# Norm halves, the place of the attention visits and the late stores in a fused attention and MLP kernel

## The chip, the cores and the metric

The kernel runs on one core of a Trainium2 chip. A core has TensorE (PE, matrix products into PSUM), VectorE (DVE), ScalarE (ACT), GpSimd (POOL) and a queue SP that issues the DMAs here. Each engine works through its own queue strictly in order. The metric is the device time of one execution in microseconds (us); lower is better.

## The reference

```python
q_n, k_n = rmsnorm(q, g_q), rmsnorm(k, g_k)       # over D = 64
attn = softmax(q_n @ k_n^T / sqrt(D))             # B, H, S, D = 8, 12, 448, 64
x = (attn @ v) as (B * S, H * D)                  # 3584 x 768
h = x @ w_in                                      # 768 -> 2048
out = (h - tanh(h)) @ w_out                       # 2048 -> 768
```

All of it is in float32; the weights come as float64 and are rounded on the chip.

## The kernel before

**Two streams.** `bounded_path` mixes two streams of work on PE. The attention goes by *slots*, one for each pair of heads: 8 batches with 6 pairs give the slots s = 0 to 47. The MLP is a Python generator `mlp()` that yields after each matmul. A slot calls `run(ns)` between its own steps, which advances the generator by so many planned nanoseconds. So the order of all the work is written out by hand: what is emitted first stands first in each engine's queue.

**The visit.** In slots s >= 12 (`slot`), PE does the attention in one block, called a visit here. `scores(s + 1, KF)` (L568) starts it: 8 matmuls into two of the three score banks (`sc`). Then `visit` interleaves the products of probabilities and values of slot s (L634, L622, into two banks of their own) with the other scores of slot s + 1. Each pair of score banks is read by two exponentials on ACT (L574), into `p_last` first, then `p` and `p_full`. As only three banks rotate, the second bank of the first full score block is the bank that the first `p_last` exponential must have read. `divide` takes the values out: an ACT copy (L754), a DVE add (L755) and a DVE multiply by the reciprocal sums (L756).

**The rest of a slot** is the list `work` of 14 points, with a stretch of MLP before each. For slot s + 1: the probabilities are added up (L599, L605, L612), transposed in 32x32 blocks and reduced (`fold`, `fold_rest`: L709, L716), brought together by eight small ACT copies (`gather`, L724), reduced, inverted, copied to the other partitions, widened and transposed (`spread_sums`, `turn_sums`: L733 to L744). For slot s + 2: q and k are scaled by their norms (L532) and transposed (L542, L546, then an ACT multiply L547). For slot s + 3: squares on ACT (L499), a reduction on DVE (L506), then the two halves of each norm, which lie in neighbouring groups of 32 partitions, are brought together (`meet_blocks`: four ACT copies L513; `meet_rest`: DVE L518 and L519). `power_blocks` (L525, POOL) takes the power -0.5 at the start of the next slot. `load_blocks` issues 8 DMAs for slot s + 4.

**The MLP by products of Strassen type.** The first layer (`hidden`) has 4 *sets* a batch. A set has seven *products* in the order 1, 5, 6, 2, 3, 7, 4, of 6 matmuls each, in three rotating PSUM banks (`mm`): 1, 5, 6 and 4 open a bank; 2, 3 and 7 add to the banks of 1, 5 and 6. In `done_with`/`use`, product 1 is copied out by ACT (L899); 5 and 6 are added to that copy by DVE (L901, L903); product 2 gets a tanh (ACT) and a subtraction (DVE, L880); 3 (L911), 7 (L907, L908) and 4 (L915) are added by DVE, and their tanh (L879) and subtraction (POOL, L880) are emitted after the next product. A bank can be opened again only when its last reader is done.

From batch 2 on two batches go together: `hidden(b)`, two *outer blocks* of `project_pair`, `hidden(b + 1)`, the other five. An outer block is seven products of 4 matmuls and a whole product of 8 double ones: 44 units of the size of one matmul. Before it, POOL makes the operands `u` (L1040) from the first layer's results; after it, DVE combines the results (L1089, the whole one of some blocks by ACT, L1096), partly at once and partly from the list `calm`, one entry a product. In `x_sums` POOL (L788) makes operands `tt` for the first layer from the attention's output.

**The phase.** A slot beside `hidden` has 42 units, one set; the slots beside the first two outer blocks have 44 and beside the others 110. So each visit falls at the same place of a set, and `AHEAD_NS`, added up over the six slots s = 12 to 17, sets that place: 6 units, so that the visit stands after product 1. A pair's slots begin at s = 18, 30 and 42.

**The stores.** `store` transposes a finished piece on DVE (L940) into a buffer `th`, of which there are two, shared with the tanh; the four output DMAs (L945) are issued on SP a product later.

Of the kernel before, what the change touches and what calls it, by code (L numbers as in the profile page):

```python
# [9 lines left out]
F32 = mybir.dt.float32  # L10
# [134 lines left out]
def bounded_path(tc, ctx, q, k, v, moe_w_in, moe_w_out, out, g_col, ident, ones, half_ones, neg_half, early):  # L145
# [20 lines left out]
    P = 128  # L166
# [320 lines left out]
    def load_blocks(s):  # L487
        b, hp = steps[s]
        t = loaded["qk", s] = qk_rows()[:, : 2 * S].rearrange("p (i j d) -> p i j d", i=2, j=NJ)
        for i, src in enumerate((q, k)):  # L490
            for h in range(2):
                rows = src[b, 2 * hp + h].rearrange("(j t) (m d) -> m t j d", t=BL, d=BL)
                for m in range(2):
                    r = (2 * h + m) * BL
                    nc.sync.dma_start(out=t[r : r + BL, i], in_=rows[m])
# [13 lines left out]
    def meet_blocks(s):  # L509

        mine, other = normed["rr", s]
        for g in range(P // BL):
            nc.scalar.copy(out=other[g * BL : (g + 1) * BL], in_=mine[(g ^ 1) * BL : ((g ^ 1) + 1) * BL])  # L513

    def meet_rest(s):

        mine, other = normed["rr", s]
        nc.vector.tensor_tensor(out=mine, in0=mine, in1=other, op=ALU.add)  # L518
        nc.vector.tensor_scalar(out=mine, in0=mine, scalar1=1.0 / D, scalar2=1e-6, op0=ALU.mult, op1=ALU.add)  # L519
        normed["rr", s] = mine  # L520

    def power_blocks(s):

# [79 lines left out]
    def add_third(s):  # L603
        for t in sums[s]:
            nc.vector.tensor_tensor(out=t, in0=t, in1=full(s)[2], op=ALU.add)  # L605
# [122 lines left out]
    def spread_sums(s):  # L728

        acc = whole[s]  # L730
        total = late["blocks"].tile([P, NJ], F32, name="sum_all")
        top = total[: 2 * BL]
        nc.vector.reduce_sum(top, acc.rearrange("p g j -> p j g"), axis=AX.X)  # L733
        nc.vector.reciprocal(top, top)
        for m in range(2):
            nc.vector.tensor_copy(out=total[(2 + m) * BL : (3 + m) * BL], in_=total[m * BL : (m + 1) * BL])
        wide = whole[s] = late["blocks"].tile([P, NJ, BL], F32, name="sum_w")
        nc.vector.tensor_copy(out=wide, in_=total[:, :, None].to_broadcast([P, NJ, BL]))

    def turn_sums(s):  # L740

        wide = whole[s]
        rs = whole[s] = late["blocks"].tile([P, S], F32, name="rs_T")
        nc.vector.transpose(out=rs, in_=wide.rearrange("p j k -> p (j k)"))  # L744

    def divide(s, av):
        b, hp = steps[s]
        rs = whole.pop(s)
        if b > PAIRED and b % 2 and hp == 1:
            x = xT[b, hp] = late["blocks"].tile([P, S], F32, name="xT_more", bufs=1)  # L750
        else:
            x = xT[b, hp] = xp.tile([P, S], F32, name="xT")
        if s >= FOLDED:
            nc.scalar.copy(out=x, in_=av[0][:, :S])  # L754
            nc.vector.tensor_tensor(out=x, in0=x, in1=av[1][:, :S], op=ALU.add)  # L755
            nc.vector.tensor_tensor(out=x, in0=x, in1=rs, op=ALU.mult)  # L756
        for m in range(2):
            rows = slice(m * D, (m + 1) * D)
            for n in range(0 if s >= FOLDED else 2):
                nc.vector.tensor_tensor(  # L760
                    out=x[rows, n * HS : (n + 1) * HS], in0=av[n][rows, :HS], in1=rs[n * D : (n + 1) * D],
                    op=ALU.mult,
                )
        for c in range(NCH):
            del probs[s, c]
        if b < PAIRED and hp >= HC:
            c = hp - HC
            x_sums(b, (c,), range(4), nc.vector if b == 0 and c == HC - 1 else nc.gpsimd)

    def x_sums_later(s, second):  # L770
        b, hp = steps[s]
        for c in {(HC + 1, 0): (0,), (HC + 1, 1): (1,), (HC + 2, 0): (2,)}.get((hp, second), ()):
            x_sums(b, (c,), range(4), nc.gpsimd)

    def x_sums(b, chunks, which, eng):
# [22 lines left out]
    def part(name):  # L798
        return tp.tile([P, 2, HS], F32, name=name)
# [131 lines left out]

        return products(b, 0, SETS, 2, HC, moving, done_with)

    def store(b, n, y):

        o = part("th").rearrange("p f s -> p (f s)")
        nc.vector.transpose(out=o, in_=y if b >= FIRST else y.rearrange("r (c p) -> r p c", c=NCH))  # L940

        def issue():
            for i in range(P // BL):
                d = n * P + i * BL
                nc.sync.dma_start(  # L945
                    out=out[b * S : (b + 1) * S, d : d + BL].rearrange("(j t) d -> t j d", t=BL),
                    in_=o[i * BL : (i + 1) * BL].rearrange("t (j d) -> t j d", d=BL),
                )

        late["out"].append([1 if b >= PAIRED else 2, issue])  # L950
# [103 lines left out]
    def project_pair(b, ks):  # L1054
# [36 lines left out]
        def combine_outer(p, m, y):  # L1091

            e, f = acc[:, m], acc2[:, m]
            if p in (1, 3):
                if m == HC - 1:
                    nc.scalar.copy(out=e if p == 1 else f, in_=y)  # L1096
                return
            third = m == HC - 1
            o = y
            if third and p in (2, 5, 4):  # L1100
                o = f if p == 2 else e if p == 4 else part("s1").rearrange("p f s -> p (f s)")

            def soon(*args):
                if third:
                    add(*args)
                else:
                    calm.append(lambda: add(*args))

            if p == 2:
                soon(o, y, e)  # L1110
                calm.append(lambda: store(b, m, o))
            elif p == 7:
                soon(e, e, y)
                soon(f, f, y, ALU.subtract)
            elif p == 6:
                soon(e, e, y)
            elif p == 5:
                soon(o, y, e)
                calm.append(lambda: add(f, f, o))
                calm.append(lambda: store(b + 1, HC + m, o))  # L1120
                calm.append(lambda: store(b + 1, m, f))
            else:
                soon(o, y, e)
                calm.append(lambda: store(b, HC + m, o))

        def flush():
            now, late["todo"] = late["todo"], []
# [168 lines left out]

    H_NS = 4 * HS / ENGINE_NS * 7 * 6 * SETS
    O_NS = 4 * HS / ENGINE_NS * 7 * HC * HF
    AHEAD_NS = 4 * HS / ENGINE_NS * 6
    OUTER_NS = 4 * HS / ENGINE_NS * (7 * HF // 2 + 2 * HF)  # L1300

    def gap_ns(s):
# [8 lines left out]
    def has(s):  # L1311
        return 0 <= s < NS
# [69 lines left out]
    def slot(s):  # L1382

        gap = gap_ns(s)
        av = av_banks
        if has(s + 1):
            scores(s + 1, KF)
        if s < FOLDED:
            last_values(s, av)
            totals(s, sc_bank())  # L1390
            divide(s, values(s, av))
            for c in range(KF):
                scores(s + 1, c)
        else:
            visit(s, av)
        if has(s + 2):
            load(s + 2, "v")
        rows, ahead, following = has(s + 2), has(s + 3), has(s + 1)
        folded = following and s + 1 >= FOLDED
        first = s + 3 == TURNED  # L1400
        scaled = rows and not first
        if scaled:
            power_blocks(s + 2)
        work = (
            ((following, lambda: add(s + 1, False)), (first, lambda: turn(s + 2, sc_bank(), sc_bank()))),
            ((following, lambda: add_third(s + 1)), (first, lambda: load_blocks(s + 3))),
            ((following, lambda: add_last(s + 1)), (first, lambda: load_blocks(s + 4))),
            ((folded, lambda: fold(s + 1)),),
            ((folded, lambda: fold_rest(s + 1)), (True, lambda: x_sums_later(s, 0))),
            ((scaled, lambda: scale_blocks(s + 2)),),  # L1410
            ((scaled, lambda: turn_blocks(s + 2, 0)), (folded, lambda: gather(s + 1, 0))),
            ((scaled, lambda: turn_blocks(s + 2, 1)), (folded, lambda: gather(s + 1, 1))),
            ((True, lambda: x_sums_later(s, 1)), (has(s + 4) and not first, lambda: load_blocks(s + 4))),
            ((folded, lambda: spread_sums(s + 1)), (ahead, lambda: square_blocks(s + 3))),
            ((folded, lambda: turn_sums(s + 1)),),
            ((ahead, lambda: norm_blocks(s + 3)),),
            ((ahead, lambda: meet_blocks(s + 3)),),
            ((ahead, lambda: meet_rest(s + 3)),),
        )
        for point in work:  # L1420
            run(4 * gap / (len(work) + 1))
            for wanted, fn in point:
                if wanted:
                    fn()
        run(4 * gap / (len(work) + 1))
# [358 lines left out]
```

## Time and profile before

| What | Value |
|---|---|
| Time, median of 3 runs | 1405.35 us (1402.68 to 1407.94) |
| Profiled execution | 1405.19 us |
| Its span (first to last instruction) | 1403.3 us |
| PE busy | 1340.1 us, 95% |
| DVE / POOL / ACT busy | 1014.8 / 720.1 / 535.9 us |
| Mean granted TensorE clock | 0.990 |
| DMA share, 250 to 440 us / 440 to 1230 us | 0.90 / 0.58 |

A row of the timeline has the start in us, the time taken in us, engine, line, operation, what is written and read, and how many; in brackets stands how long the engine was idle before it and what ended that. A row of the waits names the waiting instruction and what it waited for, then the total in us, how often, and the longest. A stretch of the windows view lists the busy time of PE, the weight loads, DVE, ACT and POOL, then the granted clock, the DMA share and GB/s. In the profile a float32 matmul of the MLP appears as two records. PE counts as busy while matmuls are in its pipeline, so short stalls do not all show as idle time.

### The profile page before, as it was taken

What the parts mean: (1) busy time and instruction counts of PE and PEld (TensorE: products, weight loads), DVE (VectorE), ACT (ScalarE), POOL (GpSimd) and SP (SyncE); (2) the same over time, 40 slices, a digit from 0 to 9 for tenths busy, and PEclk for the clock granted to TensorE, in tenths of its full rate; (3) what the DMA queues carried; (4) which work ended last, traced back from release to release, by engine and by line L of the source; (5) the groups of instructions that cost most, each with busy time, mean ns of one, the idle gap of its engine ahead of it and who ended that gap; (6) DMA issues with size and microseconds to landing.
All of it is one profiled execution on the core that took longest, in us unless ns stands there. A gap on an engine that the chain in (4) does not pass through costs nothing.

```text
span 1403.3 us, 29144 instructions
## 1 busy us (share of the span) xinstructions
PE 1340.1 (95%) x11336; PEld 1051.6 (75%) x11336; DVE 1014.8 (72%) x1529; ACT 535.9 (38%) x1291; POOL 720.1 (51%) x409
## 2 busy tenths in 40 slices
PE   7988999999999999999999999999999999999996
PEld 3467854488889886878767788688777788699884
DVE  5999989668656677868886777678796677634563
ACT  7856554343432534353321444344411254311100
POOL 4756666157672439243873336633596134712660
PEclk9999999999999999999999999999999999999998
DMA  7879889889998655565546766375653774455544
GB/s 172 187 213 253 264 239 242 257 258 330 298 277 237 167 152 148 135 163 146 151 119 145 192 161 166 92 178 144 164 160 99 149 196 134 125 152 177 168 140 78
DMA packets 371688, 253.54 MB, mean 181 GB/s; under 512 B 282196, under 2 KB 310228, under 8 KB 371540
## 3 DMA queue, kind: packets, MB, share of 16 engines
q1 hardware_dynamic: 371536, 251.57, 65.8%
q8 instruction: 92, 1.51, 0.4%
q14 instruction: 56, 0.46, 0.1%
q10 hardware_dynamic: 4, 0.00, 0.0%
HBM read 205.23 MB, written 46.27 MB: 179 GB/s over the span
## 4 chain that ended last, share of the span: by engine, by line
PE 65%; DVE 16%; DMA 6%; issue 4%; SPq 4%; ACT 3%; POOL 2%; DVEq 0%; ACTq 0%; POOLq 0%
PE mm L832 26%; PE mm L1082 20%; PE sc L568 8%; PE mm L1246 5%; PE sc L634 4%; DMA out_dram<-th 2%; DMA qk_nat<-in_q_dram 1%; DVE qk_n L532 1%; DVE rows L605 1%; DMA w_f<-w_inner 1%; DVE rr_mine L506 1%; DMA gT<-in_moe_w_in_dram 1%; PE sc L672 1%; SPq L945 1%; DVE w_out L354 1%
## 5 line engine op out<-in xcount | busy, mean ns | idle before, releaser
L832 PE MATMUL mm<-xT,w_f 128*128 128x224 f32 x1296 | 264.0, 353 | 4.1 <-DVE s L1089 3.9
L832 PEld LDWEIGHTS mm<-xT,w_f 128*128 128x128 f32 x1296 | 244.5, 190 | 10.2 <-DVE s L1089 5.4
L568 PE MATMUL sc<-qT,kT 64*32 64x448 f32 (+1 forms) x3072 | 223.5, 502 | 15.6 <-ACT p_last L574 14.4
L832 PE MATMUL mm<-tt,w_f 128*128 128x224 f32 x1044 | 209.5, 355 | 0.7 <-DVE g L880 0.7
L525 POOL TENSOR_TENSOR rr_mine<-rr_mine,neg_half 128x28 f32<-128x28 f32 x33 | 160.4, 4860 | 94.5 <-DVE rr_mine L519 42.3
L832 PEld LDWEIGHTS mm<-tt,w_f 128*128 128x128 f32 x1044 | 195.7, 190 | 16.8 <-issue 15.4
L880 POOL TENSOR_TENSOR gT<-s,th 128x448 f32<-128x448 f32 x60 | 73.4, 1225 | 193.7 <-ACT th L879 193.7
L568 PEld LDWEIGHTS sc<-qT,kT 64*32 64x32 f32 x3072 | 76.0, 106 | 92.5 <-issue 44.6
L1082 PE MATMUL mm<-u,w_f 128*128 128x224 f32 x672 | 138.8, 358 | 4.6 <-DVE acc L1089 2.3
L1082 PEld LDWEIGHTS mm<-u,w_f 128*128 128x128 f32 x672 | 126.9, 192 | 13.5 <-issue 11.9
L880 POOL TENSOR_TENSOR g<-s,th 128x448 f32<-128x448 f32 x36 | 45.8, 1275 | 171.2 <-ACT th L879 171.2
L1082 PE MATMUL mm<-gT,w_f 128*128 128x224 f32 (+1 forms) x480 | 131.6, 427 | 0.0
L634 PE MATMUL sc<-p,v_nat 64*32 64x448 f32 x1120 | 130.9, 544 | 0.0
L1082 PEld LDWEIGHTS mm<-gT,w_f 128*128 128x128 f32 x480 | 90.9, 190 | 34.7 <-issue 34.0
L1082 PE MATMUL mm<-g,w_f 128*128 128x224 f32 (+1 forms) x360 | 100.7, 433 | 5.7 <-DVE s L1089 5.7
L755 DVE TENSOR_TENSOR xT<-xT,sc 128x448 f32<-128x448 f32 x32 | 19.8, 618 | 117.5 <-PE sc L568 72.6
L1082 PEld LDWEIGHTS mm<-g,w_f 128*128 128x128 f32 x360 | 69.0, 193 | 33.7 <-issue 26.7
L574 ACT ACTIVATE p<-sc 128x448 f32<-128x448 f32 x132 | 72.1, 546 | 37.5 <-PE sc L568 34.3
L724 ACT COPY sum_g<-sum 32x14 f32<-32x14 f32 x280 | 56.3, 201 | 78.0 <-DVE sum L716 72.1
L879 ACT ACTIVATE th<-s 128x448 f32<-128x448 f32 x96 | 55.0, 573 | 61.5 <-DVE s L907 21.2
L879 ACT ACTIVATE th<-mm 128x448 f32<-128x448 f32 x32 | 17.4, 543 | 155.7 <-PE mm L832 149.8
L1246 PE MATMUL mm<-gT,w_out 128*128 128x448 f32 x192 | 74.3, 542 | 0.0
(186 smaller groups left out, 2451.4 us busy)
## 6 DMA issues: line engine op xcount, KB each, us to landing
w_f<-w_in SPq DMA_DIRECT2D x196, 384.0 KB, 3.8
w_f<-w_inner SPq DMA_DIRECT2D x63, 512.0 KB, 3.6
w_f<-w_out SPq DMA_DIRECT2D x42, 512.0 KB, 4.1
w_raw<-in_moe_w_out_dram SPq DMA_DIRECT2D x16, 768.0 KB, 5.4
out_dram<-th SPq DMA_DIRECT2D x192, 56.0 KB, 2.7
w_in<-w_out SPq DMA_DIRECT2D x21, 384.0 KB, 5.4
qk_nat<-in_q_dram SPq DMA_DIRECT2D x132, 56.0 KB, 2.4
qk_nat<-in_k_dram SPq DMA_DIRECT2D x132, 56.0 KB, 2.3
```

Source lines behind the costliest of these rows:

```text
L354: nc.vector.tensor_tensor(out=dst, in0=x, in1=y, op=op)
L525: nc.gpsimd.tensor_tensor(out=mine, in0=mine, in1=neg_half[:, :1].to_broadcast([P, 2 * NJ]), op=ALU.pow)
L568: nc.tensor.matmul(tiles[h][i * BL : (i + 1) * BL, :n], lhsT=kT[r, c * P + at : c * P + at + BL], rhs=qT[r, first : first + n], start=True ...
L574: nc.scalar.activation(p[:, h, c if c < 2 else 0, :], tiles[h][:, :n], AF.Exp, scale=1.0 if rr is None else rr[:, 0, 2 * c + h : 2 * c + h ...
L634: nc.tensor.matmul(av[g][i * BL : (i + 1) * BL, :S], lhsT=v_nat[keys, h, c, m * BL : (m + 1) * BL], rhs=p[keys, h], start=first, stop=True ...
L724: nc.scalar.copy(out=acc[h * BL : (h + 1) * BL, g], in_=part[g * BL : (g + 1) * BL, h * NJ : (h + 1) * NJ])
L755: nc.vector.tensor_tensor(out=x, in0=x, in1=av[1][:, :S], op=ALU.add)
L832: nc.tensor.matmul(bank[:, f * HS : (f + 1) * HS], lhsT=w[:, c * width + f, :], rhs=moving[p](c), start=(first and f == 0 and c == 0), sto ...
L879: nc.scalar.activation(th, h, AF.Tanh, bias=0.0, scale=1.0)
L880: eng.tensor_tensor(out=g[:, rows, cols], in0=h, in1=th, op=ALU.subtract)
L1082: nc.tensor.matmul(bank[:, :n], lhsT=w(i), rhs=mv, start=(first and i == 0), stop=(i == len(moving) - 1), skip_group_check=not first,)
L1246: nc.tensor.matmul(bank[:, :S], lhsT=w_out_row(f, n // HC)[:, n % HC * P : (n % HC + 1) * P], rhs=g[:, f, :], start=(f == 0), stop=(f == C ...
```

## The change

- `meet_blocks`: instead of four ACT copies and one DVE add, DVE adds each group of 32 partitions to its neighbour directly, four adds into `rr_other`; the scaling follows at once. `meet_rest` is gone.
- `spread_sums`: the sums stay on 64 partitions and are no longer copied to the other 64 (two DVE copies less). The widening becomes `widen_sums`, on ACT and over 64 partitions. `divide` multiplies the two halves of x separately.
- In `work`, the squares stay beside `spread_sums`, one point sooner; the reduction and the norm halves come one point sooner in the list, and the transpose of the sums goes behind them. `load_blocks` goes one point later, the POOL sums of x move to other points, and the last point is empty.
- `AHEAD_NS` goes from 6 to 18 units: the MLP is 12 units further at each visit from s = 18 on, so that the visit stands after products 1, 5 and 6.
- `store` can be given another buffer: in block 5 every second store writes into the piece `o` that has just been stored, in block 4 (the last) every store writes into an accumulator that is no longer needed. `th` is used for the others.

```diff
         for g in range(P // BL):
-            nc.scalar.copy(out=other[g * BL : (g + 1) * BL], in_=mine[(g ^ 1) * BL : ((g ^ 1) + 1) * BL])
-
-    def meet_rest(s):
-
-        mine, other = normed["rr", s]
-        nc.vector.tensor_tensor(out=mine, in0=mine, in1=other, op=ALU.add)
-        nc.vector.tensor_scalar(out=mine, in0=mine, scalar1=1.0 / D, scalar2=1e-6, op0=ALU.mult, op1=ALU.add)
-        normed["rr", s] = mine
+            own, met = slice(g * BL, (g + 1) * BL), slice((g ^ 1) * BL, ((g ^ 1) + 1) * BL)
+            nc.vector.tensor_tensor(out=other[own], in0=mine[own], in1=mine[met], op=ALU.add)
+        nc.vector.tensor_scalar(out=other, in0=other, scalar1=1.0 / D, scalar2=1e-6, op0=ALU.mult, op1=ALU.add)
+        normed["rr", s] = other
...
-        total = late["blocks"].tile([P, NJ], F32, name="sum_all")
-        top = total[: 2 * BL]
-        nc.vector.reduce_sum(top, acc.rearrange("p g j -> p j g"), axis=AX.X)
-        nc.vector.reciprocal(top, top)
-        for m in range(2):
-            nc.vector.tensor_copy(out=total[(2 + m) * BL : (3 + m) * BL], in_=total[m * BL : (m + 1) * BL])
-        wide = whole[s] = late["blocks"].tile([P, NJ, BL], F32, name="sum_w")
-        nc.vector.tensor_copy(out=wide, in_=total[:, :, None].to_broadcast([P, NJ, BL]))
+        total = whole[s] = late["blocks"].tile([2 * BL, NJ], F32, name="sum_all")
+        nc.vector.reduce_sum(total, acc.rearrange("p g j -> p j g"), axis=AX.X)
+        nc.vector.reciprocal(total, total)
+
+    def widen_sums(s):
+
+        total = whole[s]
+        wide = whole[s] = late["blocks"].tile([2 * BL, NJ, BL], F32, name="sum_w")
+        nc.scalar.copy(out=wide, in_=total[:, :, None].to_broadcast([2 * BL, NJ, BL]))
...
-            nc.vector.tensor_tensor(out=x, in0=x, in1=rs, op=ALU.mult)
         for m in range(2):
             rows = slice(m * D, (m + 1) * D)
+            if s >= FOLDED:
+                nc.vector.tensor_tensor(out=x[rows], in0=x[rows], in1=rs, op=ALU.mult)
+                continue
...
-        for c in {(HC + 1, 0): (0,), (HC + 1, 1): (1,), (HC + 2, 0): (2,)}.get((hp, second), ()):
+        for c in {(HC + 1, 1): (0,), (HC + 1, 2): (1,), (HC + 2, 0): (2,)}.get((hp, second), ()):
...
-    def store(b, n, y):
+    def store(b, n, y, o=None):
...
-        o = part("th").rearrange("p f s -> p (f s)")
+        if o is None:
+            o = part("th").rearrange("p f s -> p (f s)")
...
-                calm.append(lambda: store(b + 1, m, f))
+                calm.append(lambda: store(b + 1, m, f, o))
             else:
                 soon(o, y, e)
-                calm.append(lambda: store(b, HC + m, o))
+                calm.append(lambda: store(b, HC + m, o, f if third else e))
...
-    AHEAD_NS = 4 * HS / ENGINE_NS * 6
+    AHEAD_NS = 4 * HS / ENGINE_NS * 18
...
-            ((following, lambda: add_third(s + 1)), (first, lambda: load_blocks(s + 3))),
+            (
+                (following, lambda: add_third(s + 1)), (first, lambda: load_blocks(s + 3)),
+                (True, lambda: x_sums_later(s, 0)),
+            ),
...
-            ((folded, lambda: fold_rest(s + 1)), (True, lambda: x_sums_later(s, 0))),
+            ((folded, lambda: fold_rest(s + 1)), (True, lambda: x_sums_later(s, 1))),
...
-            ((True, lambda: x_sums_later(s, 1)), (has(s + 4) and not first, lambda: load_blocks(s + 4))),
             ((folded, lambda: spread_sums(s + 1)), (ahead, lambda: square_blocks(s + 3))),
-            ((folded, lambda: turn_sums(s + 1)),),
+            (
+                (has(s + 4) and not first, lambda: load_blocks(s + 4)), (True, lambda: x_sums_later(s, 2)),
+                (folded, lambda: widen_sums(s + 1)),
+            ),
             ((ahead, lambda: norm_blocks(s + 3)),),
             ((ahead, lambda: meet_blocks(s + 3)),),
-            ((ahead, lambda: meet_rest(s + 3)),),
+            ((folded, lambda: turn_sums(s + 1)),),
+            (),
         )
```

## The prediction

> **What bounds the kernel now.** I read the page first, then who TensorE (PE) waited for, then the timelines around one wait. The profiled execution took 1405.19 us, 1403.3 of it span; the median shown is 1405.35, so the sum below, made against the profiled run, can be read against the median too.
>
> ```profile
> span 1403.3 us, 29144 instructions
> PE 1340.1 (95%) x11336; PEld 1051.6 (75%) x11336; DVE 1014.8 (72%) x1529; ACT 535.9 (38%) x1291; POOL 720.1 (51%) x409
> ```
>
> PE is the bound, so only its stalls can be won. The waits of PE inside 440 to 1230 us, where attention (batches 3 to 7) and the MLP pairs interleave:
>
> ```profile
> PE sc L568 <- ACT p_last L574: 13.1, 11, 2.7
> PE mm L1082 <- DVE s L1089: 5.7, 2, 2.9
> PE mm L832 <- DVE s L1089: 3.9, 2, 2.4
> PE mm L1082 <- DVE s L908: 2.0, 3, 0.7
> ```
>
> That view undercounts, since weight loads move ahead. So I took each visit in PE's timeline from its first score matmul to the next product. Visits that nothing disturbs take 5.43 us (772.34 to 777.77). Numbering visits by s, with s=18 at 440.33, those of s=19 to 46 exceed 5.43 by 33.7 us in all: 0.6 to 0.8 behind the easy sets, 1.8 to 2.2 behind the fourth, 3.6 and 5.3 at s=23 and s=35. Why, in the visit that starts at 506.42 (ACT's timeline, then PE's):
>
> ```profile
> 505.88 0.58 ACT L879 ACTIVATE th<-s 128x448 f32<-128x448 f32 x1 [0.55 <-DVE s L907]
> 507.87 0.91 ACT L513 COPY rr_other<-rr_mine 32x28 f32<-32x28 f32 x4 [1.41 <-DVE rr_mine L506]
> 508.81 0.58 ACT L879 ACTIVATE th<-s 128x448 f32<-128x448 f32 x1
> 509.29 0.51 ACT L899 COPY s<-mm 128x448 f32<-128x448 f32 x1
> 509.70 0.61 ACT L574 ACTIVATE p_last<-sc 128x224 f32<-128x224 f32 x2
> ...
> 508.00 1.24 PE L634 MATMUL sc<-p,v_nat 64*32 64x448 f32 x3
> 510.12 0.56 PE L568 MATMUL sc<-qT,kT 64*32 64x448 f32 x1 [0.88 <-ACT p_last L574]
> ```
>
> The scores were ready at 506.9, but the exps stand in ACT's queue behind four norm copies, which wait for DVE's L506, then the tanh of product 4 and the copy of product 1. PE has three score banks, needs the first one back 1.9 us into the visit, and stops.
>
> **The change, part by part.** Times are from the visit's end, V. A hidden slot holds 42 matmuls of 0.383 us (7 products of 2.3) and a visit: 21.5 us undisturbed. I lay the new order of each engine's queue with the durations of the slot that starts at 490.33.
>
> *Norm halves on DVE, sooner.* ACT loses 4 x 0.23 us and the wait before them; DVE gets four 32x28 adds for one. Not in the trace: the nearest are L518 (128x28 add, 0.19) and L736 (32x14 copy, 0.17), so 0.7 for four, net +0.5; bounds 0.2 (pipelined) and 4.3 (each as L518's worst, 1.09). I take 0.7: they now stand before product 5's add, where nothing on PE is near.
>
> *Sums.* DVE loses two copies (2 x 0.19) and the widening L738 (0.3 to 0.4); ACT gets a 64x448 copy, 0.53 as L754; the multiply by the sums becomes two of 64 rows, each priced as L756 (0.55 start to start; bounds 0.3 and, blocked like the L605 of 2.14, 1.6). Net on DVE per slot with the norm: about +0.3.
>
> *Visits behind three products.* The MLP runs 12 matmuls further before each visit from s=18 on; total PE work is unchanged. DVE in the new order: division 0.1 to 1.85; L599's add to 2.95; the tanh difference L880 at 3.05; the three sum adds 3.6 to 6.0; product 3's add 6.0; transpose and reduction 6.55 to 8.7; scaling to 9.7; product 7's two adds to 10.85; two transposes to 11.95; product 4's add to 12.5. ACT: kT 12.05, gather to 13.65, tanh, square, widening, tanh, and product 1's copy ends at 16.8. The visit starts at 16.1, and PE needs the first exp done at 18.0; it is done at 17.3. So the stall goes. What is late next is the mm banks: product 5 of the next set (11.5) needs product 7's reads, done 10.85, a margin of 0.65; product 6 (13.8) has 1.3. Before, the visit lay between and gave 5.4 us more. When POOL stretches one DVE op by a us, as in the third line here, that margin is gone:
>
> ```profile
> 491.07 0.62 DVE L756 TENSOR_TENSOR xT<-xT,rs_T 128x448 f32<-128x448 f32 x1
> 491.61 1.08 DVE L599 TENSOR_TENSOR rows<-p 128x896 f32<-128x896 f32 x1
> 493.45 2.14 DVE L605 TENSOR_TENSOR rows<-rows,p_full 128x896 f32<-128x896 f32 x1
> ```
>
> I leave 0.25 us a visit on 22 visits, 5.5 of 33.7 (bounds 0 and 12). Gain 28.2.
>
> L605 ran beside POOL's 2.67 us L1040, but L756 and L599 ran at full speed beside POOL's 4.78 us power L525 (487.23 to 492.01). The Trainium skill, "SBUF — State Buffer" (SBUF: two separate sides), says that a DVE op with two SBUF inputs and a GpSimd op that reads SBUF exclude each other for a whole instruction, which speaks against the added adds and the second multiply. By it L756 would have waited 0.94 us here for the power to end; an estimate from that is 25 us over 27 slots, and the sum would be 1408. By the rows the multiplies lose nothing beside a power, and I keep that.
>
> *Where sets meet the outer products the shift costs.* Three places, two times each.
> At s=27 and 39 the fourth set of the second batch is followed directly by products 1, 5, 6 of the third outer block. Product 6 multiplies the u made by POOL (L1040, 2.1) from the difference L880 (1.14) of product 7, whose tanh stands in ACT's queue behind the gather: 13.65 + 0.56 + 1.15 + 2.1 = 17.6 with waits. Product 6 is due at 9.2 + 3.06 = 12.3. Before, the u ended at 674.33 while the visit lasted to 677.98:
>
> ```profile
> 672.23 2.10 POOL L1040 TENSOR_TENSOR u<-g,u 128x896 f32<-128x896 f32 x1
> 674.29 1.13 POOL L880 TENSOR_TENSOR g<-s,th 128x448 f32<-128x448 f32 x1
> ```
>
> That is 5.3 us of stall, twice. Long stalls also cost clock: after the 2.85 us wait that ended at 1052.36 the windows view shows
>
> ```profile
> 1052.00:1058.00 6.00, 5.64 (x15) 5.14 (x16) 4.09 (x9) 1.19 (x5) 0.95 (x1) 0.50 0.46 126
> ```
>
> a granted clock of 0.50 for 6 us, 3.4 us lost; after the 2.8 us stall at 887 about 1.7; after those at 555 and 715 nothing. I add 2.5 to each 5.3: 15.6 in all (bounds 0 and 20). The Trainium skill, "TensorE: Matmul & The Clock Gate" (Part 1: The HAM clock gate), has the clock halved after an idle window of about 3.4 us; by that the two 2.8 us stalls should not have halved it, and they did.
> At s=22 and 34, the whole product's copy L1096 frees a bank that product 6 of the next block wants at 13.0; it now stands behind gather, square and widening and ends at 15.3: 2.3 twice, 4.6 (bounds 0 and 7).
> At s=23 and 35 the same bank waits for a DVE add behind the gather, 15.9 against 14.55: 1.35 twice, 2.7 (bounds 0 and 6).
>
> *Elsewhere outside visits.* The long outer slots lost 10.2 us: twice 3.02 at 715 and 1049, behind DVE ops of 2 to 3 us beside POOL, 0.7 for a u, and the 3.4 of clock. DVE drops 2.85 us of copies and transpose just before, and L506 moves behind the add that PE waited for; I leave 2.7, gain 7.5 (bounds 0 and 10). Five small waits on L908 and L880, 3.5 us, become 1.0: gain 2.5.
>
> *Half the late stores elsewhere.* Stores shared two th buffers, and DVE waited for their DMAs: `DVE th L940 <- DMA out_dram<-th: 31.8, 14, 7.0` in DVE's waits. PE paid 1.72 at 768 and 2.55 at 1104; with six of twelve stores a pair in finished tiles this goes: gain 4.3 (bounds 0 and 4.3). After PE's end DVE wrote its last transpose at 1395.2 after a 1.2 us wait; without the waits it can end 4 us sooner, but SP issues four DMAs a store at 0.5 us each and can hold that: gain 3 (0 to 5). The moved block loads are 8 DMAs on SP one point later; PE waited for no DMA in this stage, where DMA is 58% busy, so I price them at nothing; if that cover ended, the next slot's L499 would wait for them, a slot later. x sums moved on POOL: the last chunk's first subtraction needs no new x, so it stays ahead of product 5.
>
> Sum: 28.2 + 7.5 + 2.5 + 4.3 + 3 = 45.5 gained; 15.6 + 4.6 + 2.7 = 22.9 lost; 1405.2 - 22.6 = 1382.6, say 1383.
>
> **The rivals.**
> *Slower: DVE's bank margin.* At product 5 of each next set the two multiplies, the adds and the POOL overlaps delay product 7's reads by more than 0.65 us. Each us beyond costs 22 us. Above 1.7 us of delay the net gain is gone; at 2.4 us the time is 1383 + 22 x 1.75 = 1421. For it: the 2.14 us L605. Against: slots 19 and 21 show no such op in that stretch.
> *The visits stay held.* ACT still runs tanh, square and the new widening shortly before the exps (0.7 us margin). If DVE is 1 us later than laid, a third to a half of the visit gain stays lost: 1383 + 14 = 1397.
> *The stalls where sets meet do not bite* because tanh and u come earlier than laid: without most of the 22.9 it is 1365. Against: the queue order is fixed and the old slot shows the same gather end (13.5).
> *No change*, 1405: the wins and the new stalls cancel fully, each within its bounds.
>
> **How the numbers follow.** Forecast 0.50 (own range 1374 to 1392), visits held 0.20 (1392 to 1402), no stalls at the meeting 0.15 (1358 to 1374), no change 0.06, bank-bound 0.09. The measurement tells about 0.5%, 7 us, from no change: below 1398.3 lie 0.50 + 0.15 + 0.14 = 0.79, within 0.06 + 0.06 = 0.12, above 0.09. The range 1364 to 1402 leaves out part of the third case and all slower ones.
>
> **What would show it.** Right: visits of s=19 to 26 near 5.43 us, no wait on p_last above 0.5; L513's wait for L506 gone; PE waits of 4 to 6 us for POOL's u at two places about 330 us apart, ahead of the visits s=28 and 40; fewer waits of L940 for DMAs. Wrong: PE waiting for DVE's L907 or L908 once per set (the bank rival), or p_last still in PE's list with about 13 us.

## The result and the profile after

The changed kernel takes 1419.01 us (median of 4 runs, 1416.28 to 1419.78) against 1405.01 us; the ratio is 1.0095, with a 95% interval of 1.0072 to 1.0118. It is slower by 14 us, where 22.6 us less were forecast. The profiled execution has a span of 1417.3 us, 14.0 more than before. Its page says:

```profile
span 1417.3 us, 29026 instructions
PE 1338.8 (94%) x11336; PEld 1044.0 (74%) x11336; DVE 1063.2 (75%) x1558; ACT 525.6 (37%) x1194; POOL 720.1 (51%) x409
```

PE has no more work than before, so the 14 us are waits and slow clock. These are PE's waits inside 440 to 1260 us (lines move by 1 to 5 against before: the adds of product 7 are L906 and L907, the adds of the probabilities L595, L601 and L608, the scaling L528, the gather L720, the widening L735, the tanh L878, the whole product's copy still L1096):

```profile
PE mm L1082 <- issue: 16.7, 3, 6.5
PE mm L1082 <- POOL u L1040: 10.9, 2, 5.5
PE mm L1082 <- DVE s L907: 7.0, 5, 2.1
PE mm L1082 <- DVE s L1089: 3.0, 4, 1.0
PE mm L831 <- DVE acc L1089: 2.7, 2, 1.4
PE mm L1082 <- ACT s L1156: 2.1, 2, 1.9
```

The waits on `p_last`, 13.1 us before, are gone. In their place stand few and long waits at L1082, the outer products. The visits themselves are free: those of s=19 to 46 exceed 5.43 us by 0.6 us in all, against 33.7. ACT's timeline at the visit that starts at 512.02 shows why: its queue is through with everything else when the scores arrive.

```profile
511.42 0.57 ACT L878 ACTIVATE th<-s 128x448 f32<-128x448 f32 x1
511.89 0.51 ACT L898 COPY s<-mm 128x448 f32<-128x448 f32 x1
512.77 0.61 ACT L570 ACTIVATE p_last<-sc 128x224 f32<-128x224 f32 x2 [0.37 <-PE sc L564]
```

Where the time went is told by the distances from one visit's start to the next. The third column is what 42 or 44 units of 0.383 us and a visit of 5.43 us take:

| Slots s | Before, us | Undisturbed | After, us |
|---|---|---|---|
| Inside sets (15 slots) | 336.4 | 322.8 | 323.5 |
| 28, 29, 40, 41 (long outer slots) | 204.8 | | 194.3 |
| 21, 33, 45 (sets end, outer block 1 begins) | 70.9 | 64.6 | 78.8 |
| 22, 34, 46 (outer block 2 begins) | 70.2 | 66.8 | 93.0 |
| 23, 35 (outer block 2 ends) | 53.5 | 44.6 | 47.7 |
| 27, 39 (sets end, outer block 3 begins) | 49.4 | 43.0 | 61.2 |

The last four rows stand 61.7 us above undisturbed after the change, 25.0 before. At s=22 the timelines of DVE, ACT and PE read:

```profile
547.16 3.00 DVE L601 TENSOR_TENSOR rows<-rows,p_full 128x896 f32<-128x896 f32 x1
...
550.68 4.33 DVE L608 TENSOR_TENSOR rows<-rows,p_last 64x448 f32<-64x448 f32 x2
...
557.65 0.88 ACT L720 COPY sum_g<-sum 32x14 f32<-32x14 f32 x4 [12.95 <-DVE sum L712]
...
561.00 0.88 ACT L720 COPY sum_g<-sum 32x14 f32<-32x14 f32 x4
...
562.75 0.55 ACT L735 COPY sum_w<-sum_all 64x448 f32<-64x448 f32 x1
563.21 0.52 ACT L1096 COPY acc<-mm 128x448 f32<-128x448 f32 x1
...
563.83 3.32 PE L1082 MATMUL mm<-u,w_f 128*128 128x224 f32 x8 [6.50 <-issue]
```

PE resumes 0.1 us after L1096 has freed its bank. "issue" hides this: the view names no releaser, but nothing else ends there. L1096 had its input long before; it stands in ACT's queue behind a gather that waits 12.95 us for DVE. At s=27 it is the tanh of product 7 that stands behind the gather, and POOL's chain behind that tanh (ACT, POOL, PE):

```profile
677.44 0.88 ACT L720 COPY sum_g<-sum 32x14 f32<-32x14 f32 x4
678.34 0.58 ACT L878 ACTIVATE th<-s 128x448 f32<-128x448 f32 x1
...
679.00 1.80 POOL L879 TENSOR_TENSOR g<-s,th 128x448 f32<-128x448 f32 x1 [5.68 <-ACT th L878]
680.88 2.07 POOL L1040 TENSOR_TENSOR u<-g,u 128x896 f32<-128x896 f32 x1
...
683.00 1.49 PE L1082 MATMUL mm<-u,w_f 128*128 128x224 f32 x3 [5.46 <-POOL u L1040]
```

And at s=21 DVE's scaling, 1.1 us elsewhere, takes 2.94 beside POOL's u and holds product 7's adds, whose bank PE wants for outer product 5, the second of the block (DVE, PE):

```profile
526.28 2.94 DVE L528 TENSOR_TENSOR qk_n<-qk_nat,rr_other 128x896 f32<-128x896 f32 x1
...
529.67 0.61 DVE L907 TENSOR_TENSOR s<-mm,s 128x448 f32<-128x448 f32 x1
...
530.43 4.95 PE L1082 MATMUL mm<-u,w_f 128*128 128x224 f32 x16 [2.12 <-DVE s L907]
```

Each of the long waits is followed by slow clock. The windows view (duration; PE, weight loads, DVE, ACT, POOL; granted clock, DMA share, GB/s) has, right after the stalls at s=22 and s=27:

```profile
563.80:567.00 3.20, 3.17 (x9) 2.91 (x10) 1.45 (x7) 0.17 (x1) 1.51 (x1) 0.50 0.86 244
682.80:686.00 3.20, 3.00 (x8) 2.75 (x9) 1.93 (x1) 0.00 (x0) 3.20 (x3) 0.50 0.50 133
```

### The profile page after: what moved, and what is told of

It is laid out like the page before. It is cut to its first block, busy times and chain, and to the rows that moved or that the text cites. A ratio compares the mean times of both kernels' runs of the same rounds, so it can differ in the third digit from the quotient of the medians.

```text
span 1417.3 us, 29026 instructions
## 1 busy us (share of the span) xinstructions
PE 1338.8 (94%) x11336; PEld 1044.0 (74%) x11336; DVE 1063.2 (75%) x1558; ACT 525.6 (37%) x1194; POOL 720.1 (51%) x409
## 4 chain that ended last, share of the span: by engine, by line
PE 71%; DVE 14%; POOL 5%; issue 3%; DMA 3%; SPq 1%; ACT 1%; ACTq 0%; DVEq 0%; POOLq 0%
PE mm L831 32%; PE mm L1082 17%; PE sc L564 8%; PE mm L1246 5%; PE sc L630 5%; POOL u L1040 2%; DVE xT L756 1%; PE sc L668 1%; DVE qk_n L528 1%; PE sc L618 1%; POOL tt L787 1%; DVE rows L601 1%; DVE rows L608 1%; POOL rr_other L521 1%; DVE gT L1032 1%
## 5 line engine op out<-in xcount | busy, mean ns | idle before, releaser
L564 PE MATMUL sc<-qT,kT 64*32 64x448 f32 (+1 forms) x3072 | 214.1, 500 | 3.1 <-ACT p_last L570 1.9
L521 POOL TENSOR_TENSOR rr_other<-rr_other,neg_half 128x28 f32<-128x28 f32 x33 | 160.6, 4868 | 102.8 <-DVE rr_other L515 102.8
L1082 PE MATMUL mm<-u,w_f 128*128 128x224 f32 x672 | 146.5, 372 | 35.5 <-issue 16.7
L1082 PEld LDWEIGHTS mm<-u,w_f 128*128 128x128 f32 x672 | 132.6, 200 | 42.5 <-issue 26.7
L1082 PE MATMUL mm<-gT,w_f 128*128 128x224 f32 (+1 forms) x480 | 138.4, 442 | 2.1 <-ACT s L1156 2.1
L1082 PEld LDWEIGHTS mm<-gT,w_f 128*128 128x128 f32 x480 | 94.6, 199 | 42.6 <-issue 38.6
L564 PEld LDWEIGHTS sc<-qT,kT 64*32 64x32 f32 x3072 | 70.8, 106 | 70.8 <-issue 51.7
L630 PE MATMUL sc<-p,v_nat 64*32 64x448 f32 x1120 | 111.4, 536 | 0.0
L1082 PE MATMUL mm<-g,w_f 128*128 128x224 f32 (+1 forms) x360 | 103.1, 439 | 3.5 <-DVE s L1089 3.0
L720 ACT COPY sum_g<-sum 32x14 f32<-32x14 f32 x280 | 56.3, 201 | 121.2 <-DVE sum L712 115.6
L878 ACT ACTIVATE th<-s 128x448 f32<-128x448 f32 x96 | 55.1, 575 | 120.0 <-DVE s L910 95.1
L1082 PEld LDWEIGHTS mm<-g,w_f 128*128 128x128 f32 x360 | 69.9, 197 | 34.0 <-issue 27.8
L570 ACT ACTIVATE p<-sc 128x448 f32<-128x448 f32 x132 | 71.9, 545 | 50.6 <-PE sc L564 37.8
L514 DVE TENSOR_TENSOR rr_other<-rr_mine 32x28 f32<-32x28 f32 x132 | 70.5, 534 | 3.9
```

The source lines that it names most:

```text
L514: nc.vector.tensor_tensor(out=other[own], in0=mine[own], in1=mine[met], op=ALU.add)
L521: nc.gpsimd.tensor_tensor(out=mine, in0=mine, in1=neg_half[:, :1].to_broadcast([P, 2 * NJ]), op=ALU.pow)
L564: nc.tensor.matmul(tiles[h][i * BL : (i + 1) * BL, :n], lhsT=kT[r, c * P + at : c * P + at + BL], rhs=qT[r, first : first + n], start=True ...
L570: nc.scalar.activation(p[:, h, c if c < 2 else 0, :], tiles[h][:, :n], AF.Exp, scale=1.0 if rr is None else rr[:, 0, 2 * c + h : 2 * c + h ...
L630: nc.tensor.matmul(av[g][i * BL : (i + 1) * BL, :S], lhsT=v_nat[keys, h, c, m * BL : (m + 1) * BL], rhs=p[keys, h], start=first, stop=True ...
L720: nc.scalar.copy(out=acc[h * BL : (h + 1) * BL, g], in_=part[g * BL : (g + 1) * BL, h * NJ : (h + 1) * NJ])
```

## The experiments

**Where the visits stand, and the norm halves.** The first theory ("place"): the stalls come from where the visits stand. The rival ("turn-taking"): at s=21 the four norm adds run beside POOL's u's, each add takes turns with one POOL instruction, three u's and a subtraction (0.84, 2.02, 1.08 and 2.03 us; 0.18 for most others), so the power starts late (542.38), the u's behind it fall on L601 and L608 and stretch these. Four kernels were run beside each other, with the kernel before at 1406.61 us.

```diff
# phase6 and phase12, on the changed kernel
-    AHEAD_NS = 4 * HS / ENGINE_NS * 18
+    AHEAD_NS = 4 * HS / ENGINE_NS * 6      # 12 in phase12
# before18, on the kernel before
-    AHEAD_NS = 4 * HS / ENGINE_NS * 6
+    AHEAD_NS = 4 * HS / ENGINE_NS * 18
# copies18, on the changed kernel
-            nc.vector.tensor_tensor(out=other[own], in0=mine[own], in1=mine[met], op=ALU.add)
...
+            nc.scalar.copy(out=other[g * BL : (g + 1) * BL], in_=mine[(g ^ 1) * BL : ((g ^ 1) + 1) * BL])
...
-            ((folded, lambda: turn_sums(s + 1)),),
+            ((folded, lambda: turn_sums(s + 1)), (ahead, lambda: meet_rest(s + 3))),
```

> The changed kernel with the visits put back behind product 1 (6 units), everything else kept. Place theory (the stalls where sets meet outer blocks, 17.6 us at s=27 and 39 and about 24 us at s=22, 34 and 46, come from where the visits stand): these stalls go, the visits are held only in part because the norm copies no longer stand ahead of the exponentials, time 1375 to 1392. Turn-taking theory (the four small norm adds each take turns with one POOL u, the power -0.5 comes 5 us later, and all behind it): the stalls at s=22 and 34 stay for more than half, time 1395 to 1410.

> The changed kernel with the visits behind products 1 and 5 (12 units). Place theory: at s=27 and 39 the visit stands ahead of the product 6 that waited for u, so both stalls of 5.6 us and their 3.2 us of half clock go (17.6); at s=22 and 34 the product 6 of the second outer block still comes ahead of the visit and keeps 4 to 7 us; visits near 5.5 us; time 1395 to 1405. Turn-taking theory: no place of the visits helps at s=22 and 34, and the power is late in the same way; 1400 to 1412.

> The kernel before with only the visits put behind three products (18 units). Place theory: visits near 5.43 us, but 5 to 6 us of stall at s=27 and 39 and 2 to 6 us at s=22 and 34, with their half clock, time 1400 to 1415, above the kernel before or level with it. Turn-taking theory: without the norm adds the power is on time, the stalls at s=22 and 34 are 2.5 us or less, time 1383 to 1395.

> The changed kernel, but the norm halves brought together as before: four ACT copies and one DVE add of 128 partitions, with the scaling one point later. Turn-taking theory: the power of s=21, 33 and 45 starts about 4 us sooner, the DVE adds L601 and L608 behind it run beside it at 1.1 and 0.6 us, and the 6.7 us stalls at s=22 and 34 fall to 2.5 or less, with most of their 3.2 us of half clock: time 1395 to 1402. Place theory: the stalls stay within 1.5 us of 6.7, time 1414 to 1424.

| Kernel | Median, us | Ratio to before (95%) | Slots 21 to 23, 27 and their like, above undisturbed | Visits 19 to 46 above 5.43 |
|---|---|---|---|---|
| phase6 | 1451.74 | 1.0319 (1.0291 to 1.0347) | 50.4 us | 65.4 us |
| phase12 | 1403.97 | 0.9981 (0.9964 to 0.9998) | 40.1 us | 2.7 us |
| before18 | 1446.75 | 1.0292 (1.0264 to 1.0320) | 64.8 us | 27.9 us |
| copies18 | 1417.45 | 1.0072 (1.0044 to 1.0100) | 62.7 us | 0.1 us |

(The two last columns count a visit held at one of these slots twice.) The turn-taking theory fell with copies18: no add took turns with a u any more (the scaling of the norms, L519, did once, with 1.95 us), the power started at 540.47, 1.9 us sooner though not the 4 expected, and PE lost the same 6.49 us at the same place, for the u's now fell on the division and the first sums (DVE, then PE; L760 and L599 are L756 and L595 of the changed kernel):

```profile
544.55 3.23 DVE L760 TENSOR_TENSOR xT<-xT,rs_T 64x448 f32<-64x448 f32 x2
...
548.12 2.55 DVE L599 TENSOR_TENSOR rows<-p 128x896 f32<-128x896 f32 x1
550.77 2.78 DVE L605 TENSOR_TENSOR rows<-rows,p_full 128x896 f32<-128x896 f32 x1
...
564.48 1.83 PE L1086 MATMUL mm<-u,w_f 128*128 128x224 f32 x4 [6.49 <-issue]
```

It also shows no worth of the norm halves on VectorE by themselves: the intervals of copies18 and of the changed kernel overlap. The place theory held for the stalls of before18 (5.8 us at s=22, 5 at s=27), and phase12 lies in its range (and in that of turn-taking), though not for its reason: an outer product has 4 matmuls, so 12 units are still products 1, 5 and 6, and product 6 still waited 4.5 us for u at s=27, ahead of the visit; what fell was the wait at s=22 (6.5 to 1.6 us, 3.3 at s=34) and the slow clock. Neither theory foresaw phase6 or the time of before18. The shift alone costs 40 us and the other edits alone cost 45; together they cost 14. Why, the visit at 510.10 of phase6 shows (DVE, ACT, PE):

```profile
510.56 2.14 DVE L514 TENSOR_TENSOR rr_other<-rr_mine 32x28 f32<-32x28 f32 x4
...
512.83 0.62 DVE L914 TENSOR_TENSOR s<-mm,s 128x448 f32<-128x448 f32 x1
...
513.55 0.58 ACT L878 ACTIVATE th<-s 128x448 f32<-128x448 f32 x1 [3.17 <-DVE s L914]
...
514.44 0.61 ACT L570 ACTIVATE p_last<-sc 128x224 f32<-128x224 f32 x2
...
514.85 0.56 PE L564 MATMUL sc<-qT,kT 64*32 64x448 f32 x1 [1.93 <-ACT p_last L570]
```

With the visit behind product 1, product 4 ends only one product ahead of it. The norm step, moved sooner in the slot, now stands ahead of product 4's add L914; the tanh waits for the add, and the exponentials stand behind the tanh. So the new list doesn't suit visits behind product 1, and the old one doesn't suit visits behind three products. What in the list frees the visits at 18 units was asked by one more kernel, run with the last group below (before there 1404.74 us):

```diff
# before18_sooner, on the kernel before, with 18 units
+            ((folded, lambda: spread_sums(s + 1)), (ahead, lambda: square_blocks(s + 3))),
             ((True, lambda: x_sums_later(s, 1)), (has(s + 4) and not first, lambda: load_blocks(s + 4))),
-            ((folded, lambda: spread_sums(s + 1)), (ahead, lambda: square_blocks(s + 3))),
-            ((folded, lambda: turn_sums(s + 1)),),
             ((ahead, lambda: norm_blocks(s + 3)),),
             ((ahead, lambda: meet_blocks(s + 3)),),
-            ((ahead, lambda: meet_rest(s + 3)),),
+            ((folded, lambda: turn_sums(s + 1)), (ahead, lambda: meet_rest(s + 3))),
+            (),
```

> The kernel before with the visits behind three products and one thing more: the squares one point sooner, and the reduction and the norm halves (still four ACT copies) ahead of the transpose of the sums, as in the changed kernel. Copies of the sums, widening on VectorE, the single multiply, the stores and the sums on POOL stay as before. If the place of the norm step in the slot is what frees the visits: visits near 5.43 us, no wait of the exponentials behind L513, 1417 to 1428. Rival (VectorE must also lose the widening and the two copies): visits stay at 6.4 to 8.3 us, 1435 to 1447.

Measured: 1431.88 us, ratio 1.0196 (1.0180 to 1.0211): neither. The visits fall from 6.4 to 5.7 or 5.8 us in the first batch of a pair and from 8.2 to 7.7 in the second; there the exponentials still stand behind ACT's norm copies, which wait for a reduction that DVE reaches late:

```profile
623.77 0.92 ACT L513 COPY rr_other<-rr_mine 32x28 f32<-32x28 f32 x4 [2.92 <-DVE rr_mine L506]
624.72 0.60 ACT L574 ACTIVATE p_last<-sc 128x224 f32<-128x224 f32 x2
```

So the place of the norm step gives about half of it (1446.75 to 1431.88). The rest must come from what copies18 has besides, for its visits are free with the same four ACT copies: the widening and two copies taken off DVE stand nearest, but were not tried alone, so this stays open.

**The order of the queues where sets meet outer blocks.** If PE waits only because the copy, the tanh and the adds stand behind work that nobody needs yet, putting that work some matmuls later must free it, although DVE and POOL stay as slow. The changed kernel's list was reordered in those slots alone (n is the slot's number within a pair, 3 for s=21; the names with w_ are the entries of the list `work`: w_scale the scaling, w_turn the transposes, w_gather the gather, w_square the squares, w_widen the widening):

```diff
+        n = (s - 3 * NP) % (2 * NP) if s >= 3 * NP else -1
+        if n in (3, 9):                      # late_s21: 3; late_s27: 9
+            work = (
+                w_add, w_third, w_last, w_fold, w_fold2, (), w_scale, (w_turn0,), (w_turn1, w_gather0),
+                (w_gather1, w_square), (w_spread, w_load, w_xsums), (w_widen, *w_norm), w_meet, w_turn,
+            )
+        if n in (4,):                        # late_s22; late_all has all three
+            work = (
+                w_add, w_third, w_last, w_fold, w_fold2, w_scale, (), (), (w_load, w_xsums), (w_turn0,),
+                (w_turn1, w_gather0), (w_gather1, w_square), (w_spread, w_widen), (*w_norm, *w_meet, *w_turn),
+            )
```

> The changed kernel; in the slots s=22, 34 and 46 alone, the kT turn, the gather, the square and the widening are put some matmuls later, so that on ScalarE the copy L1096 of the whole product, which frees the bank, stands ahead of them. Queue theory (PE waits because L1096 stands behind a gather whose input comes late): the stalls of 6.67, 6.64 and 3.85 us and their 3.2, 3.2 and 1.9 us of half clock go but for 0 to 1.5 us each, time 1393 to 1400. Rival (VectorE and POOL are late in these slots whatever the order, the queue only shows it): the wait comes back a little later, at the next visit or at L1089, time 1408 to 1419.

> The changed kernel; in the slots s=27 and 39 alone, the gather comes two points later in the list, so that on ScalarE the tanh of product 7, from which POOL makes the u that product 6 waits for, stands ahead of it. Queue theory: the two stalls of 5.6 us with 3.2 us of half clock each fall to 0 to 1.5 us, time 1401 to 1406. Rival (POOL's own chain of two subtractions and a u is what takes the time): the stalls fall by less than 2 us each, time 1412 to 1419.

> The changed kernel; in the slots s=21, 33 and 45 alone, the scaling L528 comes one point later, so that VectorE's adds of product 7 (L906, L907) stand ahead of it, and the gather two points later. Queue theory: the stalls of 2.3 us on L907, the 2.0 us on the copy L1156 behind them and the slow clock after them, about 4 us a place, go to under 1.5, time 1407 to 1412. Rival (the adds are late because VectorE as a whole is late beside POOL's u): they stay above 1.5 us, time 1414 to 1420.

> All three reorderings together. Queue theory: the sum, 25.5 + 17.6 + 12 = 55 us less what is left at each place, time 1364 to 1378, which would be faster than both kernels. Rival: 1395 or more.

Run beside each other, with before at 1405.45 us ("its slots" are those that the edit reorders, in the sums of the table above):

| Kernel | Median, us | Ratio to before (95%) | Its slots, changed kernel | Its slots, here |
|---|---|---|---|---|
| late_s22 | 1393.75 | 0.9913 (0.9897 to 0.9930) | 93.0 us | 67.9 us |
| late_s27 | 1408.56 | 1.0024 (1.0010 to 1.0037) | 61.2 us | 50.0 us |
| late_s21 | 1413.00 | 1.0059 (1.0042 to 1.0076) | 78.8 us | 77.9 us |
| late_all | 1389.10 | 0.9885 (0.9869 to 0.9901) | 233.0 us | 198.2 us |

late_s22 is the clearest: 25.3 us of the 25.5 expected, with DVE's busy time unchanged (1062.4 us against 1063.2). In its timelines (DVE, ACT, PE) DVE is as slow as before, to the hundredth of a us, and PE doesn't care:

```profile
546.73 3.00 DVE L601 TENSOR_TENSOR rows<-rows,p_full 128x896 f32<-128x896 f32 x1
...
550.25 4.33 DVE L608 TENSOR_TENSOR rows<-rows,p_last 64x448 f32<-64x448 f32 x2
...
553.23 0.53 ACT L1096 COPY acc<-mm 128x448 f32<-128x448 f32 x1 [8.96 <-PE mm L1082]
...
559.88 0.67 ACT L543 ACTIVATE kT<-kT,g_col 128x448 f32<-128x448 f32 x1 [4.73 <-DVE kT L542]
...
555.15 3.27 PE L1082 MATMUL mm<-u,w_f 128*128 128x224 f32 x16 [0.44 <-POOL tt L787]
```

L1096 now waits for PE and not the reverse. late_s27 gained 10.5 us, less than the 13 to 18 expected: the wait for u fell from 5.5 to 1.8 us, but the outer product's copy L1156 now stands behind the gather, the squares and a tanh (0.85 us), and slots 28 and 40 lost 1.7 us each to L1089. late_s21, between the two ranges, only moved its wait, as the rival said, though not to POOL's u: the bank came sooner, and then PE waited 2.79 us for L1156, again behind the gather, the squares and a tanh, as ACT's and PE's timelines at s=21 of late_s21 show:

```profile
530.43 1.76 ACT L720 COPY sum_g<-sum 32x14 f32<-32x14 f32 x8
...
533.53 0.33 ACT L1156 COPY s<-mm 128x224 f32<-128x224 f32 x1
...
529.37 1.75 PE L1082 MATMUL mm<-u,w_f 128*128 128x224 f32 x8 [0.70 <-POOL gT L879]
533.91 2.65 PE L1082 MATMUL mm<-gT,w_f 128*128 128x224 f32 x9 [2.79 <-ACT s L1156]
```

The 6.0 us that late_s21 gained came from s=22, 34 and 46 (93.0 to 86.9 us), where nothing had been reordered. late_all also missed: 1389.10 lies between the 1364 to 1378 of the queue theory and the rival's 1395. The place at s=22 gave all of its part (67.9 us), those at s=21 gave nothing (80.4 us against 78.8). So late_s21 and late_s27 had moved the same work not far enough. In the next group it stands behind product 1 of the outer block too, and the stores were tried alone (before 1404.74 us):

```diff
# late_more: n in (3, 9, 4); late_more5: n in (3, 9, 4, 5)
+            scale = ((), w_scale) if n in (3, 9) else (w_scale, ())
+            work = (
+                w_add, w_third, w_last, w_fold, w_fold2, *scale, (), (w_load, w_xsums), (w_turn0,),
+                (w_turn1, w_gather0), (w_gather1, w_square), (w_spread, w_widen), (*w_norm, *w_meet, *w_turn),
+            )
# stores_th
-                calm.append(lambda: store(b + 1, m, f, o))
+                calm.append(lambda: store(b + 1, m, f))
...
-                calm.append(lambda: store(b, HC + m, o, f if third else e))
+                calm.append(lambda: store(b, HC + m, o))
```

> The changed kernel with the later order of s=22, 34 and 46 also at s=21, 33, 45 (before the first outer block) and s=27, 39 (before the third): there the scaling comes one point later and turn, gather, square and widening stand behind product 1 of the outer block, so behind its copy L1156 too. Queue theory: of what the three reorderings together left (0.9 + 2.9 us with slow clock at s=21, 33, 45; 2.0 + 1.0 + 1.9 us at s=27, 39) the waits on L1156 and the 1.9 go, about 15 us in all, time 1368 to 1380. Rival (what is late there is POOL's chain of subtraction and u, and ScalarE's order moves the wait only): 1384 to 1391.

> As the run before it, and the later order at s=23 and 35 as well, where PE waits 1.5 us for the add L1089, which stands on VectorE behind the reduction that waits for the gather. Queue theory: 3 us less than the run before it. Rival (L1089 is late for VectorE's own work): no difference, within 1 us.

> The changed kernel with all late stores through th, as before. If the other buffers are worth what the slots s=29 and 41 and the tail gained (1.5 + 2.4 + 2.2 us): 1423 to 1427, about 6 us over the changed kernel. Rival (the gain there came from the other moves): 1417 to 1421.

late_more takes 1371.02 us, ratio 0.9754 (0.9737 to 0.9771), and late_more5 **1367.32 us, ratio 0.9738 (0.9724 to 0.9753)**: faster than both kernels. late_more lies in the range of the queue theory, and late_more5 is 3.7 us below it, where 3 were expected; their intervals overlap, but the slots 23 and 35 show 3.5 us. The slots 21, 33, 45 now take 65.4 us against 64.6 undisturbed, 22, 34, 46 take 66.7, 23, 35 take 44.5 and 27, 39 take 50.6; of the 61.7 us above undisturbed, 53.4 are gone. Not all of it need be the order: DVE's busy time fell too, from 1063.2 to 1047.6 us, for instance L601 at s=22, which now began before POOL's u, took 1.09 us instead of 3.00. How much that gave was not tested. What remains in late_more5 is, in its page and in PE's waits of 440 to 1240 us:

```profile
PE 1320.0 (97%) x11336; PEld 1032.0 (76%) x11336; DVE 1047.6 (77%) x1558; ACT 525.3 (38%) x1194; POOL 725.0 (53%) x409
...
PE mm L1082 <- POOL u L1040: 5.3, 2, 2.7
PE mm L1082 <- DVE s L1089: 4.1, 6, 1.0
```

stores_th takes 1420.27 us, ratio 1.0118 (1.0103 to 1.0133), 1.3 us over the changed kernel with overlapping intervals: the rival. DVE's waits for the output DMAs, none in the changed kernel, are back with 28.3 us, but of the two waits of PE that the prediction put down to them (1.72 us at 768, 2.55 us at 1104) only 0.7 us comes back, at 1126. At the end DVE finishes 3.0 us sooner in the changed kernel (1407.3 against 1410.3), but the spans, 1417.3 and 1418.3, differ by 1.0.

## Why the prediction was wrong

**The visits: right.** 28.2 of 33.7 us were to go; 33.1 went, with ACT's queue empty in time as laid.

**The outer slots and the stores: near in sum, not in the parts.** 7.5 for the long slots and 4.3 for store waits were to be gained; slots 28, 29, 40 and 41 gained 10.5, of which 1.3 belongs to held visits and 9.1 to these terms. But stores_th puts the stores at 1.3, tail included, which is within the noise. So the waits of DVE for output DMAs were long but nearly free, and most of the gain at the long slots came from the other edits.

**The failed step is "Where sets meet the outer products the shift costs", sized 22.9 us and measured as 56.2.** The last four rows of the table stand 61.7 us above undisturbed, 61.2 of it outside the visits. Before, they stood 25.0 above, but 20.0 of that were held visits, which the prediction counts by themselves, so 5.0 outside. The shift added 61.2 less 5.0. That is 33.3 us more than forecast and turns 1382.6 into 1415.9. The other terms together came out 3 us worse: the visits 4.9 us better, the long slots and stores 2.7, the small waits 2.0 and the tail 0.9 worse, and 2.5 us lost ahead of s=18 had no term. By places (waits counted from one matmul's start to the next, 0.17 us more than the idle time in the rows):

- s=27 and 39: 5.3 of wait and 2.5 of slow clock forecast, 5.6 and 2.9 measured (16.3 in all against 15.6). Mechanism and size were right, the waits for POOL's u came where the prediction had put its sign (at 683 and 1024 us), and late_s27 confirms the queue as the cause of most of it.
- s=22 and 34: the mechanism was right (L1096 behind the gather), 2.3 was forecast, 6.7 and 2.8 of half clock measured. The gather's end was laid at 13.65 us behind the visit and came at 18.3 (561.88 less 543.56). The laying gave the adds L601 and L608 2.4 us, as without a u beside them, although the slot it drew on had one (L605 2.14 us); beside the u's they took 7.3. Half clock was not priced here at all, though the prediction had read 3.4 us of it behind a wait of 2.85 us in the trace of before.
- s=46: the same bank, 3.85 of wait and 1.7 of half clock, 5.6 in all (2.2 before). "Two times each", in the prediction, was wrong: the third pair has this place too.
- s=21, 33, 45: not priced; 14.2 measured, 0.8 before. The prediction had "Five small waits on L908 and L880, 3.5 us, become 1.0" as a gain. With the visit gone from between, outer product 5 came 5.4 us sooner to product 7's bank. The margin of 0.65 us was worked out for sets that follow sets, and not for this meeting; there it went to one stretched L528.
- s=23 and 35: 1.35 each forecast, 1.5 measured; late_more5 shows the gather behind it, with 3.5 us for the two.

The rival with a time of 1421 was not what happened, and that its number lies near the measured one is chance: no slot inside a set waits for L906 or L907. The sentence drawn from the Trainium skill, "SBUF — State Buffer" (SBUF: two separate sides), with its 1408, warned in the right direction. The trace agrees with the rule beside u (L601 3.00, L528 2.94 us) and not beside the power: the multiplies L756 that began beside it in the changed kernel took 0.62 us each. But late_s22 shows that at s=22 the stretching alone didn't cost the time: it did so through a queue in which something urgent stood behind it.

## What to carry to other kernels

When a block of work is shifted against another, lay every queue again at each place where the neighbour changes, and not only in the regular slot: the gain is won many times in small pieces, and the loss comes at a few places in long ones, with slow clock behind them. On an in-order engine, first ask what stands ahead of the instruction that frees a bank; here moving work that nobody needed yet behind it turned +14 us into -37, 25 of it at one kind of place with DVE and POOL as slow as before (late_s22). An edit of a list and an edit of a phase can each be worse alone than both together, so neither is to be judged by itself.

## What the runs showed of the hardware

Beside POOL, small adds can each last as long as a POOL instruction. In the changed kernel at s=21, L514's four adds of 32x28, 0.18 us each in most other places, took 6.07 us, each lasting until the POOL instruction beside it was over (DVE, then POOL):

```profile
536.02 6.07 DVE L514 TENSOR_TENSOR rr_other<-rr_mine 32x28 f32<-32x28 f32 x4
...
534.74 2.07 POOL L1040 TENSOR_TENSOR u<-gT 128x896 f32<-128x896 f32 x1
536.78 2.08 POOL L1040 TENSOR_TENSOR u<-gT,u 128x896 f32<-128x896 f32 x1
538.83 1.15 POOL L879 TENSOR_TENSOR gT<-s,th 128x448 f32<-128x448 f32 x1
539.94 2.10 POOL L1040 TENSOR_TENSOR u<-gT 128x896 f32<-128x896 f32 x1
```

Over the whole run the 132 adds took 70.5 us of DVE, 2.1 for four; 0.7 for four was forecast, which made no measurable difference to the time (copies18). The 33 single adds of 128x28 of copies18 took 17.6 us.

The same wait does not always cost the same clock. In late_more5 both waits of 2.67 us for u (s=27 and 39) are followed by these windows:

```profile
662.70:666.00 3.30, 3.12 (x16) 3.13 (x17) 2.05 (x1) 1.96 (x6) 3.30 (x4) 1.00 0.83 196
981.40:985.00 3.60, 3.42 (x12) 3.18 (x13) 2.35 (x1) 1.96 (x6) 3.60 (x4) 0.67 0.83 203
```

One kept a granted clock of 1.00, the other fell to a mean of 0.67: cut finer, the same view gives 1.00 from 981.40 to 982.60 and 0.50 from 982.65 to 986.00, so the half clock began a microsecond after the wait had ended. The Trainium skill, "TensorE: Matmul & The Clock Gate" (Part 1: The HAM clock gate), gives an idle window of about 3.4 us that runs freely. The unequal outcome fits a window that runs freely, but a wait shorter than 3.4 us was enough here, and one of 2.12 us at s=21 of the changed kernel (0.50 from 531.70 to 535.05); after the longer waits at s=22 and 27 the clock was 0.50 both times.
